# Window keys copied side by side: one product of 120 columns in place of products of 96 and 24, and one buffer for v in place of two

## The chip, the cores and the metric

One Trainium2 chip, of which the kernel uses one core. The metric is device time in microseconds (us) of one launch; lower is better. All arithmetic is float32 or, in the large products, a float32 value split into a rounded high part and a remainder.

## The reference

Attention over short windows and block summaries, then a gated layer. Cut to what is computed:

```
B, H, S, D = 4, 8, 768, 64;  block, window = 32, 16;  nb = S // block = 24
k_sum = k.reshape(B, H, nb, block, D).max(axis=3)
v_sum = v.reshape(B, H, nb, block, D).mean(axis=3)
scores_l = q @ k.T / 8           where |i - j| < 16, else -1e9
scores_s = q @ k_sum.T / 8 + log(32)
a = softmax(concat([scores_l, scores_s]))       # + 1e-9 in the divisor
attn = a @ concat([v, v_sum])                   # (B, H, S, D)
x = attn as (3072, 512)
h = x @ w_in            # 512 -> 2048
out = (h * cos(h)) @ w_out      # 2048 -> 512
```

## The kernel before

The 3072 rows are cut into eight blocks of 384 rows (half a batch entry each). The attention of a block is done in four groups, a to d, of two heads each, so that a2 is the first group of block 2 and d7 the last group of all. The layer is done in 128 steps, s0 to s127: one step takes one slice of 128 hidden columns for one block of 384 rows. The weights stay in SBUF from block 0 on.

A group cuts its 384 queries into six tiles of 64. A tile sees 96 keys (its own 64 and 16 on either side) and the 24 block summaries, so 120 columns. The steps of a group in blocks 2 to 7, with the names that stand in the order:

- `q`, `k`, `m`, `v`: loads by DMA, all issued by SP. `m` (line 493, two DMAs) writes the v summaries and `v` (lines 477 and 485, three DMAs) the v windows, into the tile `vn`.
- `qt`, `kt`, `ks`: VectorE turns q into `qd` and k into `kd`, and writes the 24 block maxima behind the keys into `kd`. `kd` is one tile for each of the four pairs of heads and is kept over both blocks of a batch entry; k is loaded and turned in the even blocks alone.
- `sc` (line 569): the scores. For each of six tiles and two heads there are two products with the same 64 queries as weights: one with 96 columns of keys, one with the 24 summaries, in two banks of PSUM.
- `z` (580), `mx` (588), `su` (593, GpSimd), `ex` (606, ScalarE), `sm` (609), `iv` (614), `nm` (617, GpSimd): scale and mask, then the softmax; without further name these run on VectorE.
- `pt` (640), `po` (648), `pi` (655): the probabilities are turned in squares of 32, written to DRAM as `pd` by one DMA and read back by four DMAs in turned order into the tile `pt`, of which there is one buffer. The groups a2 and b2 turn theirs on TensorE instead.
- `va` (line 670): the values, twelve products of 64 columns with `vn` as weights and `pt` as the moving side. `xh` and `xl` then split the result into high and low part.

A step of the layer is `up` (line 714, twelve products of 384 columns), then on ScalarE and VectorE `tu` (724), `re` (727), `si` (732), `sq` (735), `ga` (739), then `hi` (350 or 352) and `lo` (356), then `dh` and `dl` (line 770, six and three products of 512 columns).

All five engines' queues are written out by hand: the long string `ORDER` is a list of such names (`b3.sc.4.6` is step `sc` of group b3 with banks 4 and 6; a trailing a, v or p names the engine), and each name puts its instructions behind those before it on each engine that it uses. A queue is worked in that order; between engines only the data and the buffers make one wait for another. The tile `vn` has two buffers in blocks 2 to 7, used in turn by the groups:

```
vn0 = [const.tile([NK, U, P], F32, name=f"vn{i}") for i in range(2)]
groups.append([Group(blk, i, vn0[i % 2], sc0[:, i % 2]) for i in range(NG)])
```

So the loads `m` and `v` of a group wait for the values `va` of the group two before it.

Of the kernel before, what the change touches and what calls it, by code (L numbers as in the profile page):

```python
# [52 lines left out]
s6.lo.p b2.m s7.hi.a s10.up.3 s8.tu w6.lb s7.lo.p w12.ab.0 s8.re v1_4.s.p s11.up.6 w6.fb.1 s8.si s8.sq s9.tu s8.ga  # L53
v1_5.l w6.hi.a w12.cl.v s6.dh.4.5.7 w11.l s9.re w6.lo.p w12.sh.0.1 s9.si a2.m s6.dl s8.hi.a s7.dh s9.sq s5.st.1 s9.ga
s8.lo.p s5.st.0 w12.lb s7.dl s8.dh v1_5.s.p s10.tu s9.hi.a s10.re w12.fb.1 s10.si s8.dl s10.sq s12.up.2 v1_6.l
w11.ab.0 s9.lo.v w15.l s10.ga w12.hi.a w11.cl.v s13.up.3 w11.sh.0.1 s11.tu w12.lo.p s10.hi.a s11.re s9.dh w11.lb
s11.si s11.sq s10.lo.p s11.ga s9.dl w11.fb.1 v1_6.s.p s12.tu s10.dh w15.ab.0 s12.re w13.l s14.up.6 s11.hi.a w15.cl.v
s12.si v1_7.l s11.lo.v b2.v s12.sq s13.tu s12.ga s10.dl s13.re s12.hi.a s11.dh w15.sh.0.1 w11.hi.a s12.lo.p w11.lo.p
s11.dl s14.tu w15.lb s13.si s12.dh w13.ab.0 s14.re s12.dl v1_7.s.p w15.fb.1 s13.sq s15.up.2 s14.si s13.ga s14.sq
s13.hi.a s14.ga a2.k w13.cl.v s13.lo.p s16.up.3 s14.hi.a w15.hi.a w13.sh.0.1 w15.lo.p s15.tu w13.lb s17.up.6 s15.re  # L60
w13.fb.0 s15.si s14.lo.p s13.dh s15.sq s16.tu w14.l s13.dl s16.re s15.ga a2.tk.0.0 s16.si a2.tk.1.1 s15.hi.v s16.sq
s14.dh a2.ks.0 s15.lo.p b2.k a2.ck.1.a a2.ks.1 a2.ck.0.a s16.ga s17.tu a2.sc.2.1 w13.hi.a s17.re s18.up.0 a2.z.1.v
w13.lo.p a2.z.0.v b2.qt w14.ab.1 a2.mx s14.dl s17.si w14.cl.v a2.su s15.dh s16.hi.a w14.sh.2.3 s17.sq s15.dl s17.ga
s16.lo.p a2.ex s16.dh w14.lb s16.dl w14.fb.0 s18.tu s19.up.1 s17.hi.a a2.sm w14.hi.a s17.lo.p a2.iv s18.re s17.dh
a2.nm b2.kt.0 s18.si b2.kt.1 w14.lo.p s17.dl b2.ks.0 c2.k a2.tp.0.6 b2.ks.1 s18.sq b2.sc.2.3 a2.cp.0.a s18.ga s19.tu
a2.tp.1.0 c2.q s20.up.6 b2.z.0.v a2.cp.1.a b2.z.1.v s18.hi.v s19.re s18.lo.p s19.si s21.up.2 s20.tu s19.sq s20.re
b2.mx s20.si s22.up.0 s19.ga b2.su c2.kt.0 s19.hi.v b2.ex s23.up.3 c2.kt.1 s19.lo.p c2.ks.1 d2.k s20.sq b2.sm s18.dh
s21.tu s21.re b2.iv s18.dl s21.si c2.qt s19.dh c2.ks.0 d2.q s20.ga s20.hi.v s21.sq c2.sc.1.6 s20.lo.p s21.ga a2.va.2
s22.tu s21.hi.a s19.dl d2.kt.0 c2.v s22.re s20.dh s21.lo.p c2.z.0.v a2.xh.v b2.nm s23.tu s20.dl d2.kt.1 s22.si d2.ks.1
s21.dh s22.sq d2.qt s23.re a3.q s21.dl s22.ga s23.si s24.up.1 d2.ks.0 s21.ta.1.1.a c2.z.1.v s23.sq s22.hi.v  # L70
s21.ta.2.0.v s22.lo.p b2.tp.0.0 c2.mx b2.tp.1.5 d2.sc.6.7 b2.cp.1.a b2.cp.0.v c2.su s24.tu a2.xl b2.va.5 s24.re
s25.up.0 d2.z.0.v b2.xh.a d2.m a3.qt s24.si b2.xl c2.ex s21.st.1 d2.z.1.v s26.up.2 c2.m s23.ga s23.hi.v d2.mx s23.lo.p
s24.sq s21.st.2 c2.sm s27.up.6 v2_0.l d2.su s25.tu c2.iv s24.ga c2.nm s25.re s22.dh.5.7.3 s25.si s22.dl s24.hi.v
# [36 lines left out]
s59.hi.a d4.iv c4.pi s60.re d4.nm a5.sc.2.5 s60.si s58.dh d4.pt.1 b5.qt s60.sq d4.po s58.dl a5.z.1.v c5.q s60.ga  # L110
s59.dh a5.z.0.v s60.hi.a s59.lo.v c4.va.5 s62.tu s60.lo.v s61.tu b5.sc.3.2 d4.pi s61.re a5.mx s59.dl s61.si s61.sq
s60.dh s62.re a5.su c4.xh.a b5.z.1.v a5.m s62.si s61.ga s63.up.2 s62.sq b5.z.0.v s61.hi.a a5.v b5.mx a5.ex s61.lo.p
# [71 lines left out]
def tile_kernel(  # L184
# [244 lines left out]
    class Group:  # L429
# [101 lines left out]
        def k_summaries(self, half, eng=None):  # L531
# [3 lines left out]
            if eng is None:  # L535
                nc.vector.tensor_reduce(
                    out=out, in_=self.kT[half].rearrange("p (n t) -> p n t", t=BLOCK), axis=AX.X, op=ALU.max
                )
                return
# [418 lines left out]
```

## Time and profile before

| what | value |
|---|---|
| three runs | 661.78, 663.58, 663.86 us (median 663.58) |
| profiled execution | span 660.1 us, its own time and the only one listed for it |
| TensorE matmuls (PE) | busy 632.6 us, 96% of the span, 5141 records |
| weight loads (PEld) | busy 560.2 us |
| VectorE (DVE) / ScalarE (ACT) / GpSimd (POOL) | busy 449.7 / 363.9 / 221.8 us |
| DMA | 72.68 MB, q1 busy 40.9% of 16 engines' span |
| granted TensorE clock | 0.987 |

The runs' times go from 1.7 to 3.8 us above the span, which runs from the first to the last instruction. A product of float32 stands in the trace as two records, one of float32r as one. Busy time of PE is the union of records that overlap, so a busy PE can still be done sooner by other shapes. SPq is the queue of SP, in which the DMAs are issued; its rows show how long an issue takes, not when the data land.

### The profile page before, as it was taken

The numbers are of one execution on the slowest core, as the hardware profiler recorded it, in microseconds if no ns is written. First come the engines' busy times: TensorE is split into PE (matmuls) and PEld (weight loads), VectorE is DVE, ScalarE is ACT, GpSimd is POOL, SyncE is SP. The second block draws the span as 40 slices with busy tenths as digits, with TensorE's granted clock in tenths as the row PEclk, the third lists the DMA queues.
The fourth block names the chain that finished last, engine by engine and source line by source line (L and its number), as shares of the span: only waits on it lengthen the run. The fifth ranks groups of instructions, "written<-read, shape, count | busy, mean of one in ns | idle before, by whom it ended". The sixth has DMA issues, their size and how long they took to land.

```text
span 660.1 us, 13282 instructions
## 1 busy us (share of the span) xinstructions
PE 632.6 (96%) x5141; PEld 560.2 (85%) x5141; DVE 449.7 (68%) x798; ACT 363.9 (55%) x640; POOL 221.8 (34%) x219
## 2 busy tenths in 40 slices
PE   6478999999999999999999999999999999999996
PEld 5256889989988998898898899889889989899985
DVE  4887999887855576668797777576876756433344
ACT  2656977776554485437477464356554645444342
POOL 4784896764430342301323411112330212010110
PEclk9869999999999999999999999999999999999999
DMA  9997906544243244525445433424364332000001
GB/s 224 259 271 203 276 15 223 169 109 71 55 122 85 91 124 132 127 59 114 111 107 135 147 98 97 114 43 85 115 163 104 92 94 70 5 1 17 16 17 48
DMA packets 167158, 72.68 MB, mean 110 GB/s; under 512 B 136824, under 2 KB 155832, under 8 KB 167096
## 3 DMA queue, kind: packets, MB, share of 16 engines
q1 hardware_dynamic: 167096, 71.84, 40.9%
q8 instruction: 40, 0.66, 0.4%
q14 instruction: 22, 0.18, 0.1%
HBM read 53.72 MB, written 15.73 MB: 105 GB/s over the span
## 4 chain that ended last, share of the span: by engine, by line
PE 86%; DMA 5%; SPq 3%; POOL 2%; DVE 1%; issue 1%; ACT 1%; DVEq 0%; POOLq 0%; ACTq 0%
PE banks L770 39%; PE banks L714 39%; PE banks L569 4%; PE banks L670 3%; DMA late<-in_moe_w_out_dram 3%; DMA late<-in_v_dram 1%; SPq L456 1%; POOL w L356 1%; DMA late<-in_q_dram 1%; POOL gl L356 1%; SPq L493 1%; POOL stage L393 0%; ACT stage L388 0%; PE banks L556 0%; DVE m L588 0%
## 5 line engine op out<-in xcount | busy, mean ns | idle before, releaser
L714 PE MATMUL banks<-xh,w 128*128 128x384 f32 x1024 | 272.1, 337 | 0.1
L770 PE MATMUL banks<-w,gh 128*128 128x512 f32 x768 | 198.1, 393 | 0.2 <-ACT gh L350 0.2
L714 PEld LDWEIGHTS banks<-xh,w 128*128 128x128 f32 x1024 | 185.9, 188 | 2.8 <-ACT pt L350 0.4
L714 PE MATMUL banks<-xl,w 128*128 128x384 f32 x512 | 171.4, 335 | 0.0
L770 PEld LDWEIGHTS banks<-w,gh 128*128 128x128 f32 x768 | 142.6, 188 | 29.0 <-ACT gh L350 0.5
L724 ACT ACTIVATE t<-banks 128x384 int32<-128x384 f32 x128 | 62.5, 489 | 133.6 <-DVE gl L356 54.9
L356 POOL TENSOR_TENSOR gl<-t,gh 128x384 fp32r<-128x384 f32 x55 | 56.6, 1029 | 221.4 <-ACT gh L350 86.0
L770 PE MATMUL banks<-w,gl 128*128 128x512 f32 x384 | 109.8, 394 | 0.1
L727 DVE SCALAR_TENSOR_TENSOR t<-t,banks 128x384 f32<-128x384 int32 x128 | 70.0, 548 | 56.9 <-ACT t L724 56.2
L732 ACT ACTIVATE t<-t 128x384 f32<-128x384 f32 x128 | 66.7, 523 | 66.3 <-DVE t L727 66.0
L714 PEld LDWEIGHTS banks<-xl,w 128*128 128x128 f32 x512 | 96.1, 188 | 1.6
L739 DVE SCALAR_TENSOR_TENSOR t<-t,banks 128x384 f32<-128x384 f32 x128 | 69.3, 546 | 41.2 <-ACT t L735 41.0
L770 PEld LDWEIGHTS banks<-w,gl 128*128 128x128 f32 x384 | 71.1, 188 | 14.6 <-DVE gl L356 0.2
L593 POOL TENSOR_TENSOR sc<-sc,m 128x720 f32<-128x720 f32 x28 | 40.1, 1431 | 129.2 <-DVE m L588 129.2
L735 ACT ACTIVATE t<-t 128x384 f32<-128x384 f32 x128 | 65.8, 521 | 2.1
L617 POOL TENSOR_TENSOR sc<-sc,r 128x720 f32<-128x720 f32 x28 | 39.5, 1411 | 51.4 <-DVE r L614 50.3
L350 ACT CAST gh<-t 128x384 fp32r<-128x384 f32 x68 | 34.7, 510 | 33.2 <-PE banks L770 16.5
L356 DVE TENSOR_TENSOR gl<-t,gh 128x384 fp32r<-128x384 f32 x73 | 41.7, 572 | 12.6 <-ACT gh L350 6.5
L356 POOL TENSOR_TENSOR w<-stage,w 128x1024 fp32r<-128x1024 f32 x15 | 36.2, 2416 | 10.0 <-ACT w L350 8.6
L352 DVE CAST gh<-t 128x384 fp32r<-128x384 f32 x60 | 23.2, 386 | 22.2 <-PE banks L770 20.4
L580 DVE SCALAR_TENSOR_TENSOR sc<-banks,mask 128x360 f32<-128x360 f32 x48 | 24.4, 524 | 19.2 <-PE banks L569 19.0
L569 PEld LDWEIGHTS banks<-kd,qd 64*64 64x64 f32 x1344 | 28.4, 135 | 9.4 <-issue 6.7
(102 smaller groups left out, 620.7 us busy)
## 6 DMA issues: line engine op xcount, KB each, us to landing
pd<-stage SPq DMA_DIRECT2D x22, 384.0 KB
late<-in_moe_w_in_dram SPq DMA_DIRECT2D x16, 512.0 KB
late<-in_moe_w_out_dram SPq DMA_DIRECT2D x16, 512.0 KB
pt<-pd SPq DMA_DIRECT2D x66, 96.0 KB
vn<-in_v_dram SPq DMA_DIRECT2D x52, 120.0 KB
out_dram<-stage SPq DMA_DIRECT2D x23, 256.0 KB
kn<-in_v_dram SPq DMA_DIRECT2D x24, 192.0 KB
qn<-in_q_dram SPq DMA_DIRECT2D x92, 48.0 KB
```

The lines of the kernel that those rows point to most:

```text
L350: eng.copy(out=out, in_=in_)
L356: eng.tensor_tensor(out=lo, in0=src, in1=hi.bitcast(F32), op=ALU.subtract)
L569: nc.tensor.matmul(out=self.sp[hh][s * QT : (s + 1) * QT, c, lo : lo + n], lhsT=self.qd[rows, t * QT : (t + 1) * QT], rhs=self.kd[rows, ke ...
L593: nc.gpsimd.tensor_tensor(out=self.sc, in0=self.sc, in1=self.m.unsqueeze(2).broadcast_to([P, U, NK]), op=ALU.subtract)
L617: nc.gpsimd.tensor_tensor(out=self.sc, in0=self.sc, in1=self.r.unsqueeze(2).broadcast_to([P, U, NK]), op=ALU.mult)
L714: nc.tensor.matmul(out=self.h, lhsT=w_of(name, self.f)[:, c * P : (c + 1) * P], rhs=x_of(self.blk, part, c), start=n == 0, stop=n == last,)
L724: nc.scalar.activation(out=self.t.bitcast(I32), in_=self.h, func=AF.Copy, scale=1.0 / TWO_PI)
L727: nc.vector.scalar_tensor_tensor(out=self.t, in0=self.t.bitcast(I32), scalar=-TWO_PI, in1=self.h, op0=ALU.mult, op1=ALU.add)
L732: nc.scalar.activation(out=self.t, in_=self.t, func=AF.Sin, scale=0.5)
L735: nc.scalar.activation(out=self.t, in_=self.t, func=AF.Square, scale=math.sqrt(2.0))
L739: nc.vector.scalar_tensor_tensor(out=self.t, in0=self.t, scalar=-1.0, in1=self.h, op0=ALU.add, op1=ALU.mult)
L770: nc.tensor.matmul(out=self.acc[i], lhsT=g[:, i * P : (i + 1) * P], rhs=w_of(name, self.f), start=self.first and n == 0, stop=self.last an ...
```

## The change

From block 2 on, a new step `kw` on VectorE copies a group's keys for all six tiles side by side into a tile `kw` of 128 x 6 x 120: the 96 keys of each tile by one instruction (neighbouring tiles share 32 keys, which are copied twice), and the 24 summaries behind each of the six by a second one. The scores `sc` are then one product of 120 columns for each tile and head. The tile `kw` lies in the second buffer of `vn`, so `vn` has one buffer in blocks 2 to 7, and all loads `m` and `v` from block 2 on are moved in the order to stand behind `va` of the group just before. The v summaries get two buffers, a scratch tile is renamed, and an unused branch goes.

```diff
-    kmax = const.tile([P, NB // 2, BLOCK // 2], F32, name="kmax")
+    part_sum = const.tile([P, D], F32, name="part_sum")
-    vn0 = [const.tile([NK, U, P], F32, name=f"vn{i}") for i in range(2)]
+    vn0 = [const.tile([P, U, P], F32, name=f"vn{i}") for i in range(2)]
+    kw = vn0[1].rearrange("p u n -> p (u n)")[:, : U * NK].rearrange("p (u n) -> p u n", u=U)
+    vn0 = [t[:NK] for t in vn0]
...
-            vsum[b, hg] = att.tile([P, D], F32, name=f"vs{hg}")[: HG * NB]
+            vsum[b, hg] = att.tile([P, D], F32, name=f"vs{hg}", bufs=2)[: HG * NB]
...
+        def windows(self, eng):
+
+            self.kw = kw
+            wide = bass.AP(self.kd.tensor, self.kd[:, self.base :].offset, [self.kd.ap[0], [QT, U], [1, W]])
+            copy(eng, kw[:, :, :W], wide)
+            copy(eng, kw[:, :, W:], self.kd[:, KW:].unsqueeze(1).broadcast_to([P, U, NB]))
...
         def scores(self, *two):
             if not self.masks:
                 self.score_banks(two)
+            if self.kw is not None:
+                for t in range(U):
+                    c, s = divmod(t, 2)
+                    for hh in range(2):
+                        rows = slice(hh * D, (hh + 1) * D)
+                        nc.tensor.matmul(
+                            out=self.sp[hh][s * QT : (s + 1) * QT, c, :],
+                            lhsT=self.qd[rows, t * QT : (t + 1) * QT], rhs=self.kw[rows, t, :],
+                            start=True, stop=True,
+                        )
+                return
...
-        groups.append([Group(blk, i, vn0[i % 2], sc0[:, i % 2]) for i in range(NG)])
+        groups.append([Group(blk, i, vn0[0], sc0[:, i % 2]) for i in range(NG)])
...
+            ck="place_k", ks="k_summaries", kw="windows", ms="place_masks", sc="scores", z="scale", mx="maximum",
```

Of the order string one line before, and what stands there now:

```diff
-s14.dh a2.ks.0 s15.lo.p b2.k a2.ck.1.a a2.ks.1 a2.ck.0.a s16.ga s17.tu a2.sc.2.1 w13.hi.a s17.re s18.up.0 a2.z.1.v
+s15.lo.p b2.k a2.ck.1.a a2.ks.1 a2.ck.0.a a2.kw.v s16.ga s17.tu w13.hi.a s17.re a2.sc.2.1 s18.up.0 a2.z.1.v w13.lo.p
```

Three places of the queues show what moves. The rows are those of the built program; x12 stands for twelve like instructions.

On PE (TensorE), the scores of a2 before: the products of 96 and 24 columns alternate, twelve of each, of which the first six rows are shown (`kd_99` is the key tile of pair a).

```order
L569 MATMUL banks<-kd_99,qd 64x96
L569 MATMUL banks<-kd_99,qd 64x24
L569 MATMUL banks<-kd_99,qd 64x96
L569 MATMUL banks<-kd_99,qd 64x24
L569 MATMUL banks<-kd_99,qd 64x96
L569 MATMUL banks<-kd_99,qd 64x24
```

And now (`vn_104` is the second `vn` buffer, which holds `kw`):

```order
L519 MATMUL banks<-ident,kn 128x128 x6
L782 MATMUL banks<-w_885,gh 128x512 x6
L569 MATMUL banks<-vn_104,qd 64x120 x12
L726 MATMUL banks<-xh_1_827,w_1331 128x384
L726 MATMUL banks<-xl_1_901,w_1331 128x384
```

Twenty-four products have become twelve at the same place between the same neighbours.

On DVE (VectorE), around the key summaries of a2 before, `ks` in the second row, `ga` of step s16 in the third, `re` of s17 in the fourth:

```order
L352 CAST gh<-t 128x384
L536 TENSOR_REDUCE kd_99<-banks 128x12 x2
L739 SCALAR_TENSOR_TENSOR t<-t,banks 128x384
L727 SCALAR_TENSOR_TENSOR t<-t,banks 128x384
L580 SCALAR_TENSOR_TENSOR sc<-banks,mask 128x3x120 x2
```

And now:

```order
L356 CAST gh<-t 128x384
L538 TENSOR_REDUCE kd_99<-banks 128x12 x2
L356 COPY vn_104<-kd_99 128x6x96
L356 COPY vn_104<-kd_99 128x6x24
L751 SCALAR_TENSOR_TENSOR t<-t,banks 128x384
L739 SCALAR_TENSOR_TENSOR t<-t,banks 128x384
L592 SCALAR_TENSOR_TENSOR sc<-banks,mask 128x3x120 x2
```

The two copies stand between the summaries and everything that came behind them, the scores of the same group among it.

On SP, around the read-back `pi` of d4 (`pd_3888` before) the queue was, from the `po` of d4 on:

```order
L648 DMA pd_3888<-stage_3884 128x768
L450 DMA qn<-in_q_dram 32x12x32 x4
L655 DMA pt<-pd_3888 32x4x192 x3
L655 DMA pt<-pd_3888 24x4x192
L493 DMA vn_103<-vs_2440 24x6x64 x2
L477 DMA vn_103<-in_v_dram 96x5x64 x2
L485 DMA vn_103<-in_v_dram 80x2x64
L450 DMA qn<-in_q_dram 32x12x32 x4
```

Here `vn_103` is loaded for a5, the group after. Now:

```order
L660 DMA pd_3755<-stage_3749 128x768
L454 DMA qn<-in_q_dram 32x12x32 x4
L497 DMA vn_103<-vs_2893 24x6x64 x2
L481 DMA vn_103<-in_v_dram 96x5x64 x2
L489 DMA vn_103<-in_v_dram 80x2x64
L667 DMA pt<-pd_3755 32x4x192 x3
L667 DMA pt<-pd_3755 24x4x192
L497 DMA vn_103<-vs_2378 24x6x64 x2
L481 DMA vn_103<-in_v_dram 96x5x64 x2
L489 DMA vn_103<-in_v_dram 80x2x64
L454 DMA qn<-in_q_dram 32x12x32 x4
```

The five loads `m` and `v` of d4 itself now stand ahead of its read-back, and those of a5 behind it, each waiting for the values of the group before.

More of the change, by code (lines that the diff above doesn't have):

```diff
@@ L57 @@
[L57 to L61, printed above, removed]
@@ new lines @@
+s33.sq s35.up.0 s32.hi.v s31.st.2 v2_1.s.v s32.lo.p a3.su s34.tu s36.up.6 s33.ga v2_2.l s34.re s34.si s34.sq s37.up.7
+s33.hi.a s33.lo.p v2_2.s.p s35.tu s32.dh.1.3.2 s35.re s34.ga s35.si s32.dl s35.sq v2_3.l s33.dh s34.hi.a s35.ga
+s31.fe.0.0 a3.ex s34.lo.p b3.mx d3.q s33.dl s35.hi.v s38.up.4 s35.lo.v s36.tu s37.tu s36.re a3.sm s36.si s34.dh a3.iv
+c3.kw.v s37.re a3.nm s31.ad.0 s34.dl s36.sq s37.si s35.dh b3.su a3.pt.1 s36.ga a3.po s35.dl s31.st.0 s36.hi.a
+c3.sc.0.5 s37.sq s36.lo.p s37.ga s39.up.6 s38.tu s37.hi.a s38.re c3.z.0.v s38.si a3.pi s37.lo.v b3.ex s40.up.7
@@ new lines @@
+s42.ga s43.tu s41.dh d3.iv s43.re s42.hi.v s43.si v2_4.s.v s42.lo.p c3.va.0 d3.m s41.dl d3.nm v2_5.l s43.sq d3.v
+s45.up.6 c3.xh.a s43.ga s44.tu d3.pt.1 c3.xl d3.po s46.up.7 v2_5.s.v s44.re v2_6.l s47.up.0 s43.hi.v s43.lo.p d3.pi
+s46.tu s42.dh s44.si s46.re s44.sq b3.xh.v s46.si s44.ga s42.dl s46.sq s44.hi.v s43.dh b3.xl s44.lo.p v2_6.s.p s45.tu
+s43.dl s45.re d3.va.5 a4.v s45.si s44.dh s45.sq d3.xh.a s45.ga s45.hi.v s44.dl d3.xl v2_7.l s45.dh s45.lo.v s46.ga
+s47.tu s46.hi.a s47.re s45.dl s47.si s46.dh v2_7.s.v s48.up.4 s46.lo.v a4.k s49.up.6 s48.tu s48.re s48.si s47.sq
@@ new lines @@
+s67.dh c5.pt.1 s70.si s67.dl s68.lo.v c5.po s68.dh s70.sq b5.xh.a s69.tu s68.dl b5.xl s69.re s72.up.1 d5.sm s69.si
+s69.sq c5.pi v3_4.s.v s73.up.3 s69.ga s69.hi.a s69.lo.v s70.ga s74.up.6 d5.iv s70.hi.a v3_5.l d5.nm s71.tu s71.re
+c5.va.2 d5.m d5.v s70.lo.v s71.si d5.pt.1 s71.sq s69.dh s72.tu s71.ga v3_5.s.v s69.dl s70.dh c5.xh.v v3_6.l s72.re
+s70.dl s71.hi.v s72.si s71.lo.v s75.up.7 c5.xl s73.tu s72.sq s73.re s72.ga s73.si s76.up.2 v3_6.s.v s72.hi.a s73.sq
+s72.lo.p s73.ga v3_7.l s74.tu s63.st.2 s71.dh d5.po s71.dl s73.hi.v s74.re s72.dh s73.lo.v v3_7.s.p s75.tu s72.dl
@@ new lines @@
+s99.ga s100.si s98.dh s100.sq d7.kw.v s100.ga s98.dl s99.hi.v s99.lo.v s99.dh c7.pt.1 s101.tu s99.dl s101.re c7.po
+s100.hi.v b7.va.2 c7.m c7.v s101.si s100.lo.p d7.sc.7.5 s102.tu s101.sq s100.dh d7.z.1.v d7.z.0.v d7.mx s100.dl
+s103.up.5 s101.ga d7.su c7.pi b7.xh.v s102.re s101.hi.v s102.si b7.xl s104.up.7 s101.lo.p d7.ex s105.up.0 s103.tu
+s102.sq s102.ga s103.re c7.va.2 d7.m d7.v s102.hi.v s103.si d7.sm s101.dh d7.iv s102.lo.v d7.nm s105.tu s101.dl
+s103.sq s102.dh c7.xh.a d7.pt.0 s102.dl s103.ga d7.po s106.up.1 s103.hi.v c7.xl s105.re s103.lo.v s105.si s107.up.5
@@ L177 @@
+s123.sq s124.re s122.dl s123.ga s125.up.1 s123.hi.a s124.si s123.lo.p s124.sq s124.ga s126.up.3 s124.hi.v s124.lo.v
+s127.up.4 s126.tu s125.tu s125.re s126.re s123.dh s126.si s125.si s123.dl s125.sq s126.sq s124.dh s125.ga s125.hi.v
+s125.lo.v s124.dl s127.tu s125.dh s127.re s126.ga s127.si s126.hi.v s127.sq s125.dl s126.lo.v s126.dh s127.ga
+s127.hi.a s126.dl s127.lo.p s127.dh s127.dl s127.ta.2.a s127.ta.0.0.v s127.st.2 s127.tb.2.v s127.st.0 s127.ta.1.1.v
+s127.sb.2 s127.st.1
 """
@@ L264, in v_summaries @@
         if first:
-            vsum[b, hg] = att.tile([P, D], F32, name=f"vs{hg}")[: HG * NB]
+            vsum[b, hg] = att.tile([P, D], F32, name=f"vs{hg}", bufs=2)[: HG * NB]
         out_t = vsum[b, hg]
         if eng is nc.vector:
-            to = out_t if first else kmax.rearrange("p n t -> p (n t)")[: t.shape[0], :D]
+            to = out_t if first else part_sum[: t.shape[0]]
             eng.tensor_reduce(out=to, in_=t.rearrange("p (j d) -> p d j", d=D), axis=AX.X, op=ALU.add)
@@ L529, in place_k, with k_summaries @@
             copy(eng, self.kd[:, c0 : c0 + TB], self.kT[half])
-        def k_summaries(self, half, eng=None):
+        def k_summaries(self, half):
             n = NB // 2
-            out = self.kd[:, KW + half * n : KW + (half + 1) * n]
[L535 to L539, printed above, removed]
-            c0 = WINDOW + half * TB
-            t, w = self.kd[:, c0 : c0 + TB].rearrange("p (n t) -> p n t", t=BLOCK), BLOCK
-            while w > 2:
-                w //= 2
-                to = kmax[:, :, :w]
-                eng.tensor_tensor(out=to, in0=t[:, :, :w], in1=t[:, :, w : 2 * w], op=ALU.max)
-                t = to
-            eng.tensor_tensor(out=out, in0=t[:, :, 0], in1=t[:, :, 1], op=ALU.max)
+            nc.vector.tensor_reduce(
+                out=self.kd[:, KW + half * n : KW + (half + 1) * n],
+                in_=self.kT[half].rearrange("p (n t) -> p n t", t=BLOCK), axis=AX.X, op=ALU.max,
+            )
[4 more added lines that the diff above has]
+            copy(eng, kw[:, :, W:], self.kd[:, KW:].unsqueeze(1).broadcast_to([P, U, NB]))
         def score_banks(self, two):
@@ L562, in scores @@
                 self.score_banks(two)
+            if self.kw is not None:
[7 more added lines that the diff above has]
+                            start=True, stop=True,
+                        )
+                return
             for t in range(U):
```

211 lines of the change are left out of this document (96 added, 115 removed).

## The prediction

> **What bounds the kernel now.** I read the page first, then its engines by stretch.
>
> ```profile
> span 660.1 us, 13282 instructions
> PE 632.6 (96%) x5141; PEld 560.2 (85%) x5141; DVE 449.7 (68%) x798; ACT 363.9 (55%) x640; POOL 221.8 (34%) x219
> PE 86%; DMA 5%; SPq 3%; POOL 2%; DVE 1%; issue 1%; ACT 1%; DVEq 0%; POOLq 0%; ACTq 0%
> sum 448.00, PE 448.00 PEld 401.30 DVE 310.06 ACT 245.40 POOL 120.46; mean PE 64.00 PEld 57.33 DVE 44.29 ACT 35.06 POOL 17.21
> 300.00:360.00 60.00, 60.00 (x635) 53.32 (x634) 48.07 (x92) 38.75 (x62) 17.87 (x14) 1.00 0.49 119
> ```
>
> The last two rows are busy times by stretch: the sum from 132 to 580 us, and the stretch in which VectorE (fourth number) is fullest. All groups that the change touches lie between 132 and 580 us, and PE is busy there in 448.00 of 448.00 us. So PE is the bound: what it saves there shortens the run, and each wait that it gets lengthens it by its whole length. VectorE works 310 of the 448 us, at most 48.07 of 60.
>
> What scores and values take on PE, by shape and by the chain of waits:
>
> ```profile
> L569 PE MATMUL banks<-kd,qd 64*64 64x96 f32 x672 | 29.0, 268 | 0.0
> L569 PE MATMUL banks<-kd,qd 64*64 64x24 f32 x672 | 24.8, 200 | 0.0
> L670 PE MATMUL banks<-pt,vn 120*64 120x64 f32 x624 | 24.6, 230 | 7.7 <-ACT pt L350 5.4 <-DMA vn<-in_v_dram 2.3
> 175.00 1.02 PE banks L569 x36
> 176.01 0.85 PE banks L670 x24
> ```
>
> The first three rows give one record's mean (268, 200, 230 ns), the last two start and length of one group's scores and values. A record of 24 columns lasts three quarters as long as one of 96: length goes by the record as well as by the column. The chain row leaves out some; a group's scores are 48 records.
>
> **The change part by part.**
>
> *Shorter scores.* 24 products a group become 12, in 24 groups; the columns stay (96 + 24 = 120). A 64x64 product uses a quarter of the array and the quarters overlap (48 records of 200 to 268 ns fit in 1.02 us). Each quarter gets three pairs, so 3 x 120 columns in two records each: 720 columns in 12 records. The values use halves: six products of 64 columns, two records each, 768 columns in 12 records, and that takes 0.85 us. So the columns cannot be what makes 1.02 us. At the values' rate (0.85/768 = 1.107 ns a column, start and drain in it) the new scores' 720 columns in 6 records take 0.80 us: 0.22 us less a group, 24 x 0.22 = 5.3 us. The bounds: if columns alone count, 1.02 stays and nothing is saved; if records alone count, half of them take 0.51 us, 24 x 0.51 = 12.2 us. I take 5.3, since the values are the nearest row: same number type, same kind of partial array, record lengths between the two.
>
> [...]
>
> *Two copies on VectorE.* Their nearest rows are copies of float32, from SBUF (gh, w) and from PSUM (kd, pt):
>
> ```profile
> L352 DVE CAST gh<-t x60: 310/360/1255, 73.6 to 649.7; 128x384 fp32r<-128x384 f32 x60
> L352 DVE CAST w<-stage x3: 681/740/1024, 72.7 to 99.3; 128x1024 fp32r<-128x1024 f32 x3
> L352 DVE COPY kd<-banks x2: 548/548/548, 7.7 to 15.1; 128x384 f32<-128x384 f32 x2
> L352 DVE COPY pt<-banks x1: 692/692/692, 174.8 to 174.8; 120x512 f32<-120x512 f32 x1
> ```
>
> The numbers are shortest, median and longest ns. From SBUF the slope is (740 - 360)/640 = 0.59 ns an element, so 6 x 96 = 576 elements take 0.47 us and 6 x 24 = 144 take 0.22: 0.70 us together. From PSUM it is (692 - 548)/128 = 1.125 ns, so 0.76 + 0.28 = 1.04 us, the upper bound. Source and target are SBUF, so I take 0.70. 24 x 0.70 = 17 us more VectorE work, 310 to 327 of 448 us; in the fullest stretch six groups add 4.2 to 48.07 of 60. Behind each pair of copies wait the gates and casts of the layer, which feed the products of line 770. At one place there is no cover, the scores of a2; the rows are PE and VectorE there, the same at a6, and the 768 products that wait for the casts:
>
> ```profile
> 137.87 1.62 PE L770 MATMUL banks<-w,gh 128*128 128x512 f32 x6
> 137.97 1.25 DVE L536 TENSOR_REDUCE kd<-banks 128x12 f32<-128x384 f32 x2
> 138.15 0.89 ACT L350 COPY kd<-banks 128x384 f32<-128x384 f32 x2
> 139.42 1.09 PE L569 MATMUL banks<-kd,qd 64*64 64x96 f32 x48
> 428.36 0.54 DVE L536 TENSOR_REDUCE kd<-kd 128x12 f32<-128x384 f32 x1
> 429.77 1.09 PE L569 MATMUL banks<-kd,qd 64*64 64x96 f32 x48
> L770 PE MATMUL banks<-w,gh 128*128 128x512 f32 x768 | 198.1, 393 | 0.2 <-ACT gh L350 0.2
> ```
>
> The summaries end at 137.97 + 1.25 = 139.22 and the scores begin at 139.42, only 0.2 us behind. The copies go between: PE waits 0.70 - 0.2 = 0.5 us (0.84 by the upper price, none if the copies cost 0.2). The next closest is a6, where summaries end at 428.90 and scores begin at 429.77: 0.87 us, just enough, so 0 there and elsewhere. The layer's products waited 0.2 us in all for their casts, so the casts come ahead of them; with that cover gone each group would cost up to 0.7 us.
>
> *Later v loads.* With one buffer, `m` and `v` of a group wait for `va` of the group just before, and SP works in order, so whatever stands behind them waits too. The place where least time lies between is c4 to d4:
>
> ```profile
> 352.28 0.85 PE banks L670 x24
> 353.13 1.02 PE banks L569 x36
> 354.14 2.26 PE banks L770 x9
> 356.41 2.11 PE banks L714 x12
> 358.51 0.85 PE banks L670 x24
> 353.17 1.70 SPq L655 DMA_DIRECT2D pt<-pd  x4
> 354.92 1.67 SPq L493 DMA_DIRECT2D vn<-vs  x2
> 356.63 1.05 SPq L477 DMA_DIRECT2D vn<-in_v_dram  x2
> 357.73 0.49 SPq L485 DMA_DIRECT2D vn<-in_v_dram  x1
> 354.40:355.20 0.80, 0.80 (x5) 0.66 (x4) 0.80 (x3) 0.72 (x2) 0.64 (x1) 1.00 0.78 203
> 355.20:356.10 0.90, 0.90 (x6) 0.73 (x5) 0.87 (x3) 0.84 (x2) 0.26 (x1) 1.00 0.64 179
> 356.10:356.50 0.40, 0.40 (x4) 0.36 (x3) 0.40 (x1) 0.40 (x1) 0.40 (x1) 1.00 0.13 33
> ```
>
> The chain (first five) has `va` of c4 end at 353.13 and that of d4 begin at 358.51. SP's rows: the read-back `pt` starts once c4's `va` is done (353.17) and is issued by 354.87; five loads `m` and `v`, there for the next group, take from 354.92 to 358.22, 3.3 us. In the rows by stretch the next-to-last numbers, the DMA share, stay at 0.78 and 0.64 to 356.1 and fall to 0.13: the data land about 1.2 us after the issue. Now d4's own five loads stand ahead of that read-back: it starts at 353.17 + 3.35 = 356.5, is issued at 358.2 and lands at 359.4. Before, it landed at 356.1, 2.4 us before it was needed; now PE would be ready at 358.51 - 0.22 = 358.3 and waits 1.1 us. Lower bound 0 (if issues overlap better), upper 2.8 (if a group of issues stalls once as the longest do).
>
> The next tightest places:
>
> ```profile
> 486.56 0.85 PE banks L670 x24
> 494.89 0.85 PE banks L670 x24
> 489.31 0.39 SPq L648 DMA_DIRECT2D pd<-stage  x1
> 489.80 2.33 SPq L655 DMA_DIRECT2D pt<-pd  x4
> 250.88 0.85 PE banks L670 x24
> 259.15 0.85 PE banks L670 x24
> ```
>
> From b6 to c6 PE has 494.89 - 487.41 = 7.5 us; the same sum with `po` between (3.4 + 0.5 + 2.33 + 1.2 = 7.4) just fits, and with 0.22 less on PE it costs 0.1. From a3 to b3, 259.15 - 251.73 = 7.4 us against 3.4 + 1.7 + 1.2 = 6.3: 1.1 to spare. All others have over 8 us, or the read-back is not behind the loads. Read-backs, q loads and v-block loads behind these five are late by 1.7 to 3.3 us where they moved; their users on VectorE come about that much later, so I put 0.2 on the whole and not nothing. The renamed scratch tile and the second buffer of v summaries issue nothing.
>
> *Sum*, against the profiled execution's span of 660.1 us: -5.3 + 0.5 + 1.1 + 0.1 + 0.2 = -3.4, so 656.7. The median of the three runs, 663.58, lies 3.5 above that span, and I keep that distance: 660.2.
>
> **The rivals.**
>
> [...]
>
> *SP becomes the bound* (slower). With one v buffer the chain `va`, five issues, read-back, landing, `va` must fit between two groups; 6.3 us where nothing else stands between (at d4 5.4 us are there). It turns the sign when it gets 1.8 us longer at each of the tight places, by a slower landing or issues queueing behind one another: d4 2.9, c6 1.9, b3 0.7 + 0.2 for the shorter scores, two or three places with 8 to 9 us about 0.5 each: 7.2 + 0.5 for a2 against 5.3 saved, 663.6 + 2.4 = 666.0. For it: one read-back above took 2.33 us to issue instead of 1.70, and SP holds q, po and read-backs in one order. Against it: the issues sit in most places at their common length.
>
> *VectorE's copies cost 1.04 us and push the gates onto PE.* a2 costs 0.84, d4 1.1, and some six gates with thin cover 0.25 each: -5.3 + 0.84 + 1.1 + 0.3 + 1.5 = -1.6, 662.0. Against it: 31% of VectorE is free.
>
> *Records alone count.* -12.2 + 0.5 + 1.4 + some 0.5 more wait as PE gets ahead: -9.8, 653.8. Against it: 24 columns and 96 do not last the same.
>
> **How the numbers follow.** Chances: forecast 0.56, columns alone 0.14, SP 0.14, copies 0.08, records alone 0.08. A measurement of this kernel tells about 0.3%, 2 us, from no change: faster is below 661.6, slower above 665.6. Faster: nine tenths of the forecast's 0.56 (0.50) and records alone 0.08, so 0.58; same: the rest of the forecast 0.05, copies 0.08, columns 0.13, so 0.26; slower: SP 0.14 and 0.02 of the others, 0.16. The forecast's own range is 658.4 (scores at 0.74, waits 1.5) to 662.0 (waits 3.7). Leaving out records alone and SP's upper end gives 657.0 to 665.6.
>
> **What would show it.** Right: scores of one group at 0.78 to 0.83 us in the chain; a wait of PE for kw's copy at a2 of half a microsecond; a wait of `va` of d4 for the read-back of 1 to 1.5 us; no other wait of PE above 0.5 us from 132 to 580. Wrong: scores still near 1.02, waits of `va` for vn or pt in many groups, copies over 1 us.

## The result and the profile after

| | median (lowest to highest) | ratio to before |
|---|---|---|
| before | 662.08 us (660.95 to 664.82), 17 runs | |
| changed | 667.98 us (662.65 to 670.32), 17 runs | 1.0071, interval 1.0055 to 1.0087 |

The changed kernel is slower by 0.7%, outside the forecast range of 657.0 to 665.6; that is 4.7 us by the ratio and 5.9 us by the medians. The median of three from which the forecast started, 663.58, lies 1.5 us above that of the 17 runs of the kernel before. Its profiled execution was the fastest of its 17 runs (662.65 us), so the profile shows too small a loss; further on stand two later ones at 668.63 and 669.87. Lines have moved: scores stay 569, values are 682, `up` 726, `dh` and `dl` 782, the copies 356, `re` 739, `ga` 751; the read-back is 667, `m` 497, `v` 481 and 489.

The page of the changed kernel, and the sum of its stretches from 132 to 580 us:

```profile
span 660.9 us, 12174 instructions
PE 629.8 (95%) x4565; PEld 553.5 (84%) x4565; DVE 465.9 (70%) x846; ACT 363.8 (55%) x640; POOL 221.6 (34%) x219
PE 71%; DVE 8%; DMA 6%; SPq 5%; POOL 4%; issue 3%; ACT 2%; DVEq 0%; POOLq 0%; ACTq 0%
...
sum 448.00, PE 441.50 PEld 390.66 DVE 325.30 ACT 243.31 POOL 118.66; mean PE 63.07 PEld 55.81 DVE 46.47 ACT 34.76 POOL 16.95
```

TensorE had no gap in these 448 us before; now 6.5 us are missing, and the chain that ended last runs through VectorE, DMA and SP's queue for 19% of the span instead of 9%. The wait view of TensorE names the gaps (total, times, longest):

```profile
PE banks L682 <- DMA pt<-pd: 2.0, 1, 2.0
PE banks L569 <- DVE vn L356: 1.5, 3, 1.0
PE banks L569 <- DVE t L751: 1.5, 1, 1.5
PE banks L782 <- DVE gh L356: 0.8, 1, 0.8
PE banks L682 <- DVE t L739: 0.7, 1, 0.7
```

Values at d4 wait for the read-back; scores at a2, b2 and d3 for the copies; scores at d3 again for a gate `ga`; the layer at s45 for a cast; values at c6. The last is put down to `re`, which ended 0.3 us earlier; SP's queue there has the read-back's issue end at 493.84, 2.2 us ahead, so it is taken for a second late read-back; the run with the copies made once, further on, bears that out.

Scores and copies by shape (shortest, median, longest ns):

```profile
L569 PE MATMUL banks<-vn,qd x576: 262/263/314, 138.5 to 543.6; 64*64 64x120 f32 x192
L356 DVE COPY vn<-kd x48: 222/447/1949, 137.9 to 536.2; 128x576 f32<-128x576 f32 x24, 128x144 f32<-128x144 f32 x24
```

A group's scores are 24 records instead of 48 and take 0.78 us where nothing holds them, against 1.02. The common copy takes 0.45 us (keys) or 0.23 us (summaries), and a pair 0.59 us, since the two overlap. But the longest takes 1.95 us: seven of the 48 last two to six times their length. All seven ran beside a GpSimd instruction and ended at most 0.32 us behind one; the 17 pairs that ran beside none took 0.56 to 0.60 us.

**A held copy, b2.** Timeline of the changed kernel, three engines (start, us, engine; a row may group two instructions):

```profile
149.13 2.39 POOL L360 TENSOR_TENSOR w<-stage,w 128x1024 fp32r<-128x1024 f32 x1
149.88 2.09 DVE L356 COPY vn<-kd 128x576 f32<-128x576 f32 x2
152.03 0.85 PE L569 MATMUL banks<-vn,qd 64*64 64x120 f32 x24 [0.97 <-DVE vn L356]
```

The copies start while GpSimd is at work on a weight slice and end 0.45 us behind it. TensorE waits 0.97 us.

**A held copy, d3.** The same view:

```profile
246.27 2.86 POOL L629 TENSOR_TENSOR sc<-sc,r 128x720 f32<-128x720 f32 x2 [0.96 <-ACT sc L618]
249.09 1.21 POOL L360 TENSOR_TENSOR gl<-t,gh 128x384 fp32r<-128x384 f32 x1
248.60 1.79 DVE L356 COPY vn<-kd 128x576 f32<-128x576 f32 x2
250.31 1.01 DVE L271 TENSOR_REDUCE part_sum<-kn 96x64 f32<-96x512 f32 x1
251.72 0.54 DVE L751 SCALAR_TENSOR_TENSOR t<-t,banks 128x384 f32<-128x384 f32 x1
252.32 0.84 PE L569 MATMUL banks<-vn,qd 64*64 64x120 f32 x22 [1.46 <-DVE t L751]
```

The two copies take 1.79 us instead of 0.59 and push a v summary (250.31) and the gate of s39 (251.72) back. That gate reads bank 6 of PSUM, into which d3's scores (`d3.sc.4.6`) are written: two records run, the other 22 wait until the gate ends at 252.26.

**The late read-back, d4.** SP's queue, then the end of the chain at the same place:

```profile
353.50 1.73 SPq L497 DMA_DIRECT2D vn<-vs  x2
355.28 1.05 SPq L481 DMA_DIRECT2D vn<-in_v_dram  x2
356.38 0.49 SPq L489 DMA_DIRECT2D vn<-in_v_dram  x1
356.91 1.84 SPq L667 DMA_DIRECT2D pt<-pd  x4
...
358.35 2.06 DMA pt<-pd
360.41 0.20 issue
360.61 0.92 PE banks L682 x24
```

The read-back is issued by 358.75, 0.5 us later than predicted, and its last part lands at 360.41, 1.66 us behind that; 1.2 had been taken.

**A late v block, s45.** SP's queue, VectorE, TensorE:

```profile
269.10 1.72 SPq L497 DMA_DIRECT2D vn<-vs  x2
270.92 0.47 SPq L256 DMA_DIRECT2D kn<-in_v_dram  x1
273.98 1.07 DVE L271 TENSOR_REDUCE part_sum<-kn 96x64 f32<-96x512 f32 x1 [3.13 <-DMA kn<-in_v_dram]
284.28 0.96 PE L782 MATMUL banks<-w,gh 128*128 128x512 f32 x3 [0.84 <-DVE gh L356]
```

The load of a v block (`v2_5.l`) stands behind d3's `m`, which waits for c3's values. VectorE idles 3.13 us for it; ten microseconds later the layer still waits 0.84 us for a cast.

### The profile page after: what moved, and what is told of

Read it like the earlier page. It is cut to its first block, busy times and chain, and to the rows that moved or that the text cites. A ratio compares the mean times of both kernels' runs of the same rounds, so it can differ in the third digit from the quotient of the medians.

```text
span 660.9 us, 12174 instructions
## 1 busy us (share of the span) xinstructions
PE 629.8 (95%) x4565; PEld 553.5 (84%) x4565; DVE 465.9 (70%) x846; ACT 363.8 (55%) x640; POOL 221.6 (34%) x219
## 4 chain that ended last, share of the span: by engine, by line
PE 71%; DVE 8%; DMA 6%; SPq 5%; POOL 4%; issue 3%; ACT 2%; DVEq 0%; POOLq 0%; ACTq 0%
PE banks L782 33%; PE banks L726 32%; DMA late<-in_moe_w_out_dram 3%; PE banks L682 3%; PE banks L569 3%; POOL gl L360 2%; DMA late<-in_v_dram 2%; POOL w L360 1%; SPq L460 1%; SPq L497 1%; DVE t L739 1%; DVE vn L356 1%; SPq L481 1%; DVE t L751 1%; DVE stage L419 1%
## 5 line engine op out<-in xcount | busy, mean ns | idle before, releaser
L682 PEld LDWEIGHTS banks<-pt,vn 120*64 120x64 f32 x624 | 21.0, 141 | 16.7 <-issue 8.5
L682 PE MATMUL banks<-pt,vn 120*64 120x64 f32 x624 | 24.6, 230 | 9.9 <-ACT pt L354 5.5
```

The costliest lines, as they stand in the source:

```text
L682: nc.tensor.matmul(out=self.xps[rows, t * QT : (t + 1) * QT], lhsT=self.vn[:, t, rows], rhs=self.pt[2 * c + hh][s], start=True, stop=True,)
```

## The experiments

Times are compared by the ratio to the kernel before on the same chip; its medians in the four groups of runs were 662.17, 662.38, 662.23 and 662.18 us.

### What the parts cost

**The changed kernel once more** (no edit).

> The changed kernel as it is, for a second profile, since the profiled run (span 660.9 us) was the fastest of 17 and the median run spans about 666. Theory V (one v buffer): the slower runs show longer or more waits of the values for vn or pt than the 1.98 + 0.67 us of the first profile, by some 3 to 5 us in all. Theory K (the copies on VectorE): they show longer waits of scores and gates behind the copies than the 3.8 us there. Theory T (the clock): PE's waits are the same and the granted clock is lower after 60 us, about 8 us more at half clock.

Measured: 666.74 us, ratio 1.0074 (1.0050 to 1.0098). Its profile (668.63 us) has nearly the same gaps, 7.1 us, but lies 6.0 us above the first one. Stretches of it (length, then busy us of PE, PEld, DVE, ACT, POOL with counts, then granted clock, DMA share, GB/s):

```profile
253.00:255.90 2.90, 1.44 (x25) 1.05 (x26) 2.77 (x6) 0.89 (x2) 0.40 (x1) 1.00 0.35 77
255.90:259.30 3.40, 3.40 (x9) 2.60 (x9) 2.26 (x5) 1.73 (x4) 0.60 (x1) 0.50 0.56 133
259.30:262.70 3.40, 3.40 (x17) 2.97 (x17) 1.90 (x4) 1.42 (x4) 0.86 (x1) 1.00 0.64 208
361.00:365.00 4.00, 1.98 (x13) 1.69 (x13) 2.40 (x5) 3.62 (x5) 2.36 (x2) 1.00 0.63 157
365.10:368.50 3.40, 3.40 (x29) 2.90 (x28) 2.07 (x5) 1.20 (x1) 0.00 (x0) 0.50 0.04 11
368.50:372.00 3.50, 3.50 (x19) 3.14 (x19) 2.72 (x7) 1.05 (x2) 2.25 (x2) 1.00 0.60 124
```

Right behind the waits at d3 and d4 the granted clock is 0.50 for 3.4 us, in which 9 records run where 17 run in the next 3.4 us (255.9 and 259.3). Half of each such stretch, 1.7 us, is lost. Of the rest of the 6.0 us, 2.4 us are a later start of a2's scores (140.9 against 138.5). So theory T is right in kind, with 3.4 us at stake and not 8.

**One buffer for v alone**: the changed kernel's loads and buffer, with the scores of before and no copies.

```diff
-a2.ck.0.a a2.kw.v s16.ga
+a2.ck.0.a s16.ga
```

(the same for all 24 `kw`; without `kw` the code takes the two products of before)

> The one v buffer and the moved loads alone: no copies, scores as 24 products of 96 and 24. V: slower than before by 5 to 9 us, since nothing is saved. K: slower by the waits at d4 and c6 alone, 1.5 to 3 us. T: like V if the waits at d4 lower the clock, no different in clock from before if not.

Measured: 666.34 us, 1.0071 (1.0052 to 1.0091): +4.2 us by the medians, between the two forecasts. Gaps of 0.81 (s45), 1.79 (d4) and 0.82 us (c6), and no half-clock stretch.

**Copies and scores alone**: two buffers for v, loads where they were before, and `kw` in weight slice 15, with slice 14 used in its place.

```diff
-        return wm[f][:, i * DM : (i + 1) * DM]
+        return wm[min(f, NF - 2)][:, i * DM : (i + 1) * DM]
...
+            kw = wm[NF - 1][:, 2 * DM : 2 * DM + U * NK].bitcast(F32).rearrange("p (u n) -> p u n", u=U)
...
-        groups.append([Group(blk, i, vn0[0], sc0[:, i % 2]) for i in range(NG)])
+        groups.append([Group(blk, i, vn0[i % 2], sc0[:, i % 2]) for i in range(NG)])
```

> The copies and the products of 120 columns with two v buffers and the loads in the order of before. The copies go into part of the last weight slice, for which the slice before it is used in its place, so the output is not the reference's; the work is the same. V: faster than before by 3 to 5 us (5.8 saved on scores, 1 to 3 lost to the copies). K: no faster than before, -1 to +3 us.

Measured: 659.44 us, 0.9957 (0.9945 to 0.9969): -2.7 us, with gaps of 0.41 (a2), 0.86 (b2) and 1.15 us (d3). So this half of the change was a gain, near what theory V has.

**Copies once**: kept for a2 alone; all later groups use a2's keys.

```diff
+            if (self.blk, self.pr) == (2, 0):
-            copy(eng, kw[:, :, :W], wide)
-            copy(eng, kw[:, :, W:], self.kd[:, KW:].unsqueeze(1).broadcast_to([P, U, NB]))
+                copy(eng, kw[:, :, :W], wide)
+                copy(eng, kw[:, :, W:], self.kd[:, KW:].unsqueeze(1).broadcast_to([P, U, NB]))
```

> The changed kernel with the two copies made for the first group alone; the later scores read that group's keys again, so 46 copies and the waits for them are left out. One v buffer as in the change. V: still no faster than before, about 3 us under the changed kernel at most. K: faster than before by 2 to 4 us, 8 us under the changed kernel's median.

Measured: 662.67 us, 1.0009 (0.9999 to 1.0019): 4.1 us under the changed kernel in the same group of runs, again between the two forecasts. The gaps at b2 and d3 are gone; the one at d4 has grown, since TensorE comes there sooner (first row). The second row is c6, where the wait view now names the read-back itself:

```profile
360.18 0.92 PE L683 MATMUL banks<-pt,vn 120*64 120x64 f32 x24 [2.86 <-DMA pt<-pd]
495.75 0.92 PE L683 MATMUL banks<-pt,vn 120*64 120x64 f32 x24 [1.07 <-DMA pt<-pd]
```

The two halves do not add: by the ratios +4.7 and -2.8 make +1.9, and the whole gives +4.9 here and +4.7 in the first runs. By the intervals these 3 us are uncertain by about 2. Some 1 us are longer waits (6.2 to 7.3 us behind the start of a2's scores in the changed kernel's profiles, 3.4 and 2.0 in the halves'). The half-clock stretches, which neither half's profile has, are large enough for the rest (two of them 3.4 us); this sum alone does not show that they are it.

### Taking the waits away

**The loads and values spaced**: at d4 and c6 the values go behind more of the layer, at s45 and a3 the loads go behind what had to wait for them. Of the lines of the order, the parts that change are shown, for d4, c6, s45 and a3 in turn.

```diff
-c5.qt d4.va.7 a5.m a5.v b5.su s62.ga d5.q c4.xl s60.dl d4.xh.v b5.ex s61.dh s62.hi.v
+c5.qt b5.su s62.ga d5.q c4.xl s60.dl b5.ex s61.dh d4.va.7 a5.m a5.v d4.xh.v s62.hi.v
...
-s91.si c6.va.4 d6.m d6.v s91.sq a7.ex s89.dl s91.ga
+s91.si s91.sq a7.ex s89.dl c6.va.4 d6.m d6.v s91.ga
...
-d3.m s41.dl d3.nm v2_5.l s43.sq d3.v
+s41.dl d3.nm v2_5.l s43.sq d3.m d3.v
...
-d2.va.0 a3.m a3.v b3.sc.4.6
+d2.va.0 b3.sc.4.6
-s31.fe.2.1 b3.z.1.v
+s31.fe.2.1 a3.m a3.v b3.z.1.v
```

> The changed kernel with four moves in the order: the values of d4 go behind two more pieces of the layer's products (2.2 us of PE work), those of c6 behind one (0.85 us), one load of a block of v goes ahead of d3's v summaries, and two loads of the first run's sums ahead of a3's v. Theory V: the waits at d4 (2.0), c6 (0.7) and s45 (0.9 to 1.0) go, and with the first the half clock behind it: 3 to 5 us faster than the changed kernel. Rival: the values' wait only moves, to c5's or a5's read-back, under 1 us gained.

Measured: 660.13 us, 0.9975 (0.9965 to 0.9986). The gaps at s45 and c6 are gone, d4's is 0.40 us, those of a2, b2 and d3 stay (0.30, 0.91, 1.15). Moving ten steps at four places is worth 6.6 us against the changed kernel (1.0074), and the changed kernel is then faster than before.

**The same moves without copies**: before's scores, one buffer for v.

> The kernel before with one buffer for v and no copies and with before's scores, and the loads moved as in the spaced kernel. If v's whole loss alone (4.2 us) was the few places where loads stand behind one another on SyncE's queue: within 1 us of the kernel before. If one buffer for v costs at many places, a little each: 2 us or more above it.

Measured: 663.16 us, 1.0010 (0.9998 to 1.0023), of which +0.9 us is within the uncertainty. From 132 to 580 us TensorE has no gap:

```profile
sum 448.00, PE 448.00 PEld 401.15 DVE 311.27 ACT 245.31 POOL 120.60; mean PE 448.00 PEld 401.15 DVE 311.27 ACT 245.31 POOL 120.60
```

So the loss by one buffer for v was these few places, and not a little everywhere.

### What holds the copies

**Copies with two sources**, the maximum of the keys with themselves.

```diff
-            copy(eng, kw[:, :, :W], wide)
+            eng.tensor_tensor(out=kw[:, :, :W], in0=wide, in1=wide, op=ALU.max)
```

(the summaries likewise)

> The changed kernel with each copy written as the maximum of the keys with themselves, a two-source instruction with the same result. Theory P (a one-source copy from SBUF to SBUF stands still while GpSimd runs an instruction; seven of the 48 copies took 0.85 to 1.95 us, and each ended within 0.3 us of the end of a GpSimd one): all copies last the same, 0.7 to 0.8 and 0.25 to 0.35 us, none above 1 us; the wait of b2's scores falls from 0.97 to under 0.4 us, that of d3 from 1.74 to under 0.4; a2's grows from 0.6 to about 1. Faster than the changed kernel by 1.5 to 4 us. Theory L (VectorE is simply loaded more): the longer instructions make it as slow or slower.

Measured: 668.77 us, 1.0103 (1.0077 to 1.0129), not faster than the changed kernel (1.0074), where a gain of 1.5 to 4 us had been forecast. The common lengths are 0.75 and 0.30 us, and b2's is held all the same (timeline):

```profile
151.46 2.40 POOL L360 TENSOR_TENSOR w<-stage,w 128x1024 fp32r<-128x1024 f32 x1
152.22 2.25 DVE L548 TENSOR_TENSOR vn<-kd 128x576 f32<-128x576 f32 x1
```

The theory that a copy with one source alone is held fell here: an instruction with two sources is held too. The profile has one half-clock stretch, behind d3's waits of 0.66 and 1.46 us.

**Both**: spaced, with two sources.

> The copies of f1 and the moves of f2 together. V and P: only about 1.5 us of waits are left (a2, b2), against 5.8 saved on scores, and no half clock after 62 us: 3 to 5 us faster than before, so 657 to 659. Rival (the gain is lost elsewhere whatever the waits): within 1.5 us of before.

Measured: 664.01 us, 1.0033 (1.0020 to 1.0045), where 657 to 659 had been expected. The waits at b2 (1.13) and d3 (0.33 and 1.46) stay.

**Copies and scores alone, with two sources.**

> Two v buffers, the loads in the order of before, and the two-source copies (into part of the last weight slice, so the slice before it is used in its place). P: the waits of e3 at b2 (0.86) and d3 (1.15) shrink, that of a2 grows by 0.4: 1 to 2 us faster than e3, 4 to 5 faster than before. L: as e3 or slower.

Measured: 663.10 us, 1.0013 (0.9998 to 1.0028), against 0.9957 with plain copies. A gain of 1 to 2 us over the plain copies had been expected; longer copies that are held as well take the gain away.

**Spaced, with copies by a reduction** over an axis of one element.

```diff
-            copy(eng, kw[:, :, :W], wide)
+            eng.tensor_reduce(out=kw[:, :, :W], in_=wide.unsqueeze(3), axis=AX.X, op=ALU.max)
```

(the summaries likewise; written as a loop over the two)

> [...] Rival (GpSimd holds any VectorE instruction that happens to run beside it): copies at b2 and d3 still take 1 to 2 us, and the time is about 664.

Measured: 659.61 us, 0.9953 (0.9934 to 0.9972), 0.8% under the same kernel with two sources, whose copies have the same common length. All 48 by shape, and b2 in the timeline:

```profile
L548 DVE TENSOR_REDUCE vn<-kd x48: 286/502/748, 139.0 to 532.9; 128x576 f32<-128x576 f32 x24, 128x144 f32<-128x144 f32 x24
...
150.43 2.40 POOL L360 TENSOR_TENSOR w<-stage,w 128x1024 fp32r<-128x1024 f32 x1
151.19 0.95 DVE L548 TENSOR_REDUCE vn<-kd 128x576 f32<-128x576 f32 x2
152.50 0.85 PE L569 MATMUL banks<-vn,qd 64*64 64x120 f32 x24
```

None takes over 0.75 us. At b2 both end 0.7 us before the GpSimd instruction that held them in the other kernels, and TensorE waits neither there nor at d3. At this place the form of the instruction, not the mere company of GpSimd, decides.

The longest copy of the keys took 1.95 us in the plain form, 2.25 us with two sources and 0.75 us as a reduction. Why the first two forms are held and the third is not was not shown.

**Spaced, d3's copies one step earlier**, behind the gate of s38, where GpSimd rests.

```diff
-b3.pt.1 d3.kw.v s38.hi.a
+b3.pt.1 s38.hi.a
...
-s39.tu s38.ga c3.ex
+s39.tu s38.ga d3.kw.v c3.ex
```

> The spaced kernel with d3's copies issued one step earlier, right behind s38's ga, where GpSimd has nothing running in the spaced kernel's profile. If the hold by GpSimd is what makes d3 late: both copies take 0.45 and 0.23 us there, TensorE's wait of 1.15 us before d3's scores is gone or under 0.3, and the time falls by about 1 us, to 659.1. If the wait at d3 is of the copies' own length or their place behind other work, it stays at 1 us and the time at 660.

Measured: 660.29 us, 0.9960 (0.9945 to 0.9976). d3's wait fell from 1.15 to 0.23 us; against 0.9975 the time is lower by the microsecond expected, but the intervals overlap, so the time does not show it.

**And b2's copies on ScalarE** (`b2.kw.v` becomes `b2.kw.a`).

> As the one with d3's copies early, and b2's two copies on ScalarE. By the theory of the hold TensorE waits under 0.4 us at b2 (0.91 before) and at d3, and the time is about 658.2, 4 us under the kernel before. Rival: ScalarE's copies of the same size take longer (about 0.8 us and 0.4), so that b2's wait stays near 0.9 and the time is that of the kernel with d3 early alone, 659.

Measured: 658.57 us, 0.9936 (0.9916 to 0.9957), 4.2 us under the kernel before by the ratio (3.7 by the medians) and the lowest time of all. ScalarE's two copies take 0.87 us together, beside the GpSimd instruction, and nearly no gap is left (stretch from 132 to 580 us):

```profile
sum 448.00, PE 447.07 PEld 395.48 DVE 325.92 ACT 247.03 POOL 121.16; mean PE 447.07 PEld 395.48 DVE 325.92 ACT 247.03 POOL 121.16
```

### Does a wait cost more than its length?

**d4 put back in the spaced kernel**: the first two diff lines of the spacing undone.

> The spaced kernel (660.1) with d4's values, loads and split put back where the change has them: one long wait of TensorE, of about 2 us at d4, comes back, all else stays spaced. If a wait costs itself alone: 0.40 us of wait at d4 become 2.0, so 661.7. If the clock falls to half for one stretch of 3.4 us behind a wait of that length in most runs: 1.7 us more, 663.4, and the profile shows a stretch at 0.5 behind d4's wait.

Measured: 664.06 us, 1.0023 (1.0008 to 1.0037), some 3.2 us by the ratios, as the half clock would give. But its profile shows d4's wait at 2.08 us and no half-clock stretch; in it a2 begins 1.7 us later than in the spaced kernel's, ahead of any difference between the two programs. One profile cannot speak for the twelve runs, and this one settles nothing.

**d4 put back in the spaced kernel with reductions.**

> The same put back in the spaced kernel with copies by reduce (659.6), which has no wait over 0.7 us: d4's wait of about 2 us is then the only long one. By itself 661.2; with a half-clock stretch in most runs 662.9.

Measured: 660.66 us, 0.9980 (0.9967 to 0.9993), 1.8 us above by the ratios. The one wait is

```profile
359.27 0.92 PE L682 MATMUL banks<-pt,vn 120*64 120x64 f32 x24 [2.20 <-DMA pt<-pd]
```

against 0 before the edit at that place; no half-clock stretch. Here the wait costs about itself.

**The changed kernel, a third profile.**

> The changed kernel once more, for its profile. If the half-clock stretches are what lies between its fastest run (662.65) and its median (667.98): a run near 668 shows two stretches of 3.4 us at half clock behind the waits at d3 and d4, a run near 663 none, a run near 666 one.

Measured: 669.87 us, with half clock for one stretch behind d3's wait of 1.46 us and for two in a row at the end of d4's of 2.57 us. Two rows of its stretches:

```profile
365.10:368.50 3.40, 3.40 (x29) 2.90 (x30) 1.93 (x4) 0.69 (x1) 0.00 (x0) 0.50 0.04 11
368.50:372.00 3.50, 3.50 (x12) 2.81 (x11) 2.72 (x7) 1.05 (x2) 2.10 (x2) 0.61 0.57 120
```

The three profiles of the changed kernel (0, 2 and 3 stretches) order as their times do. Taken over all profiles, a half-clock stretch followed 5 of the 14 waits of TensorE of 1.4 us or more from 132 us on, and in the seven profiles without such a wait there is none. Length alone does not decide between the 5 and the 9: waits of 2.86, 2.20 and 2.08 us are among the 9.

Where a wait falls tells more. In the trace of the kernel before and the first of the changed one all changes of the granted clock lie 3.413 us or a whole multiple of it apart (the longest 179 times it, 610.99 us); the two half-clock stretches of the second profile of the changed kernel begin 32 times it apart, at 255.9 and 365.1. So each trace is cut here into intervals of that length, with its own clock changes as borders. The rows are one such interval of the second profile of the changed kernel, ahead of a half-clock stretch, and then two in a row of the kernel with copies made once, where a border divides the wait of 2.86 us:

```profile
252.48:255.89 3.41, 1.67 (x34) 1.14 (x30) 3.28 (x7) 1.00 (x2) 0.77 (x2) 1.00 0.45 125
...
355.17:358.58 3.41, 2.15 (x13) 1.83 (x11) 1.64 (x4) 3.02 (x5) 2.00 (x2) 1.00 0.63 149
358.58:361.99 3.41, 1.81 (x28) 1.64 (x29) 0.85 (x3) 1.10 (x1) 0.00 (x0) 1.00 0.20 55
```

TensorE idled 1.74 us in the first and 1.26 and 1.60 us in the other two. From 132 to 580 us the five intervals ahead of half clock have 1.74, 1.74, 2.02, 2.03 and 2.12 us of idle time. Full clock followed the wait of 2.86 us, divided as above, and that of 1.98 us at d4 in the first profile of the changed kernel, which a border divides into 1.45 and 0.53 us; but it also followed an interval with 1.79 us (v alone, at d4). (The second half-clock interval in a row, in the third profile, follows one into which the same wait still reached for 0.55 us.) So in these cases the idle time within one interval goes with the clock in all but one. This is read from the traces afterwards; no run was made to test it, and the one exception stays open.

### The account

From the start of a2's scores to the end of the span:

| profile | us | TensorE waits in it | half-clock stretches |
|---|---|---|---|
| before | 520.7 | 0.0 | 0 |
| changed, first | 522.4 | 6.2 | 0 |
| changed, second | 525.9 | 6.5 | 2 |
| changed, third | 528.1 | 7.3 | 3 |
| v alone | 524.6 | 3.4 | 0 |
| copies and scores alone | 517.7 | 2.0 | 0 |
| spaced | 518.8 | 2.5 | 0 |
| spaced, reductions | 517.2 | 1.1 | 0 |
| spaced, d3 early, b2 on ScalarE | 516.9 | 0.6 | 0 |

Each row with the new scores is 520.7 - 5.8 + its waits + 1.7 for each stretch, and 0.8 to 1.4 us more. For the second changed profile: 520.7 - 5.8 + 6.5 + 3.4 = 524.8, measured 525.9. That remainder of about 1 us has no place of its own in the trace.

## Why the prediction was wrong, by its steps

The forecast was -3.4 us and the ratio gives +4.7. The second profile of the changed kernel (+5.2 us from the start of a2's scores on) shows where the difference lies: held copies cost about 2.7 us where nothing was put, the later loads about 2.3 us more than the sum has, two half-clock stretches 3.4 us, and about 1 us has no place. The step that failed first is the cover of the copies; the size of the later loads and the price of a wait failed beside it.

*Shorter scores* (-5.3): right. 0.78 us a group where 0.80 was predicted, 24 x 0.24 = 5.8 us, of which about 5 arrive (the account leaves 0.8 to 1.4 us). The values were the right row to price by. At their rate 1.02 us is the time of 921 columns; 576 stand in six records of 96, so each of the six records of 24 took the time of about 58 columns (an estimate from these rows). "Columns alone count" is refuted for these products: equal columns, a quarter less time (0.78 us for 1.02).

*Two copies on VectorE*, the price: right. 0.45 and 0.23 us, 0.59 together, where 0.70 was taken, and 0.30 us at a2 where 0.5 was.

*Two copies on VectorE*, the cover: this step failed. "0.87 us, just enough, so 0 there and elsewhere" went by the common duration; at b2 and d3 the copies are held by GpSimd, and TensorE waits 0.97 and 0.26 + 1.46 = 2.7 us in all where 0 stood. The quoted row `gh<-t x60: 310/360/1255` held the sign: a cast three and a half times its median. That longest one, in the trace of before, ran from 342.20 us beside a GpSimd instruction (`sc<-sc,m`) and ended 0.21 us behind it. The row was not followed to what ran beside it, and where each `kw` falls against GpSimd's queue was not looked at. The rival "VectorE's copies cost 1.04 us and push the gates" had the mechanism of d3, a gate late on PSUM, at the wrong price.

*Later v loads* (+1.1 + 0.1 + 0.2): the place at d4 was right, the size was not. d4 cost 2.0 us: the read-back's issue ended 0.5 us late, it landed 1.66 us behind that instead of 1.2, 0.2 us passed from landing to start, and TensorE was ready 0.3 us later than the sum had it. c6 cost 0.7. The "0.2 on the whole" for what stands behind the loads was one v block, 0.8 us at s45. Together 3.5 us for 1.4; measured alone, +4.2 us, of which +0.9, within the uncertainty, is left when four places are spaced.

*Not in the sum*: the clock behind the waits. By the waits alone the changed kernel's own profile would be about level (522.4 against 520.7, 1.7 us up); the two later profiles, at 668.63 and 669.87 us, have 3.4 and 5.1 us more by half clock. The sum priced a wait at its length, as its opening says ("each wait that it gets lengthens it by its whole length"); with half clock behind it, such a wait cost at least 1.7 us more than its length.

*Rivals.* "SP becomes the bound" (666.0) came nearest in number and had d4 and c6, each at a larger price than measured (2.9 and 1.9). It missed the held copies and the clock, so its number is right partly by accident.

## What to carry to other kernels

Before a copy is put on VectorE beside a busy GpSimd (here one of 0.45 us took up to 1.95), read the longest duration of its nearest rows and what GpSimd ran then; a form that is not held (here a reduction over one element, or ScalarE) can leave fewer waits than a shorter one: 1.1 us instead of 2.5 in the spaced kernel, though the intervals of the two times overlap. When a buffer is given up, list every DMA that then stands behind the moved loads on the same queue, and space those few places in the same edit: here four places decided the sign. A wait of TensorE can cost more than its length: behind waits of 1.46 to 2.6 us each half-clock stretch that followed cost 1.7 us more here.

## What was not expected of the hardware

- A VectorE copy of 0.45 us stood for 1.95 us beside a GpSimd instruction of 2.4 us, and ended within half a microsecond of its end; a reduction of the same size took no more than 0.75 us beside the same instruction.
- Waits of 1.46 to 2.6 us were followed, in some executions, by 3.4 us at a granted clock of 0.50, once by twice that; one of 2.86 us, divided by a border into 1.26 and 1.60 us, was followed by none. The five intervals of 3.41 us ahead of half clock had 1.74 us or more of idle time.
- The start of a2's scores lies between 137.9 and 142.3 us over the profiles, though little differs between the programs ahead of it; the granted clock of the first 60 us differs as well. Single profiles therefore compare only from there on.
